# Filter taps folded about the middle of n1, with the filter's first transform stage in four 64x64 tiles

## The chip, the cores and the metric

The kernel runs on one core of one Trainium2 chip. The metric is the device time of one execution in microseconds. Before the change it is 1558.56 us, the median of three runs (1558.08 to 1559.79).

## The reference

Three layers follow one another. The first is a long convolution with a filter that a small network makes; two feed-forward layers work on its result. Only the first one is touched here.

```python
h_mlp = np.maximum(pos_emb @ w1, 0.0) @ w2          # 12480 x 128
h_filt = h_mlp * np.exp(-0.01 * np.arange(S))[:, None]
u = x * v
L = 2 * S
y = np.fft.irfft(np.fft.rfft(u, n=L, axis=1) * np.fft.rfft(h_filt, n=L, axis=0)[None], n=L, axis=1)[:, :S]
x = x * y                                            # then two layers of 128 -> 2048 -> 128
```

## The kernel before, in words

A sequence position is n1 * 128 + n2. The filter has weight only at its first 82 values of n1 (NH = 82), the data at 98. The transform over n1 is a matrix multiply with cosines and sines at 90 frequencies (K1 = 90). The channels are worked on in two groups g of 64. The program up to the feed-forward layers is written out in a fixed order, which every engine's queue keeps:

1. **Filter layers** (`layer1` L450, `layer2` L464, the loop at L477). `layer1` takes six values j of n2 (a *chunk*; 11 chunks, the last of four): two TensorE calls of 492 columns, one for each half q of n2 on 64 rows of the array each (L455), then two VectorE operations with relu and window for the two halves (L458) and a GpSimd add that makes their sum (L462) into `rh`. `layer2` takes four j: eight calls, 64 rows deep, 82 values of n1 wide, 128 columns (L469), then two ScalarE copies out of PSUM (L471), to `hf` for group 0 and to `ht` for group 1. One or two `layer2` follow each `layer1`. `make_u` (L400, L403) is work on the data: one VectorE product and two sums for each of 16 blocks; two of the blocks are done between layers.
2. **first(0, 1, i)**, 16 turns (L560): the filter's first stage of group 0. A turn has eight calls of 64 weight columns and 180 moving columns (L568), in two column tiles q (64 columns of the array each), and one ScalarE copy of 720 values (L574) into `A`. Its moving operand `f1t` is the table `f1` with the window over n1, made by ScalarE at L486 after the last `layer2`. `ht` is stored to DRAM (`hsc`) behind the first turn, and the next seven `make_u` are issued between turns.
3. **first(0, 0, i)**, 16 turns, the same for the data; then the second stage of group 0 (L596 to L635: `xp`, product, `gp`), 23 blocks.
4. **first(1, 0, i)**, 16 turns; `hf` is loaded back from `hsc` behind turns 4, 7, 10, 13 (L711). **first(1, 1, i)**, 16 turns on it. Then the second stage of group 1, 23 blocks, and the feed-forward layers, which take the rest of the time.

`feed(n)` runs n steps of the conversion of the four weight matrices (L516 to L539: VectorE and ScalarE work; loads `wk<-ws`): one step in a block of the second stage, two in a turn of first(1, .).

An fp32 call of TensorE is two passes: it leaves two LDWEIGHTS and two MATMUL rows in the trace, which stand next to each other in the program, on the same part of the array. A pass of two calls that sit on different halves of the array is called a *round* below. PSUM holds three buffers of two banks in turn (`bank_b`), so TensorE is at most three tiles ahead of ScalarE or VectorE.

## Time and profile before

| | |
|---|---|
| median of 3 runs | 1558.56 us |
| profiled execution, its own time | 1559.5 us |
| its span in the trace | 1557.7 us |
| busy: PE, VectorE, ScalarE, GpSimd | 98%, 91%, 84%, 86% of the span |
| mean granted TensorE clock | 0.992 |
| instructions | 22611 |

The shares of busy time are averages over stages with different limits: the feed-forward layers fill the last four fifths of the span and hold most of each sum. What the change is worth has to be read in the stretches that it touches, which all lie in the first 266 us.

### The profile page before, as it was taken

To read this page: it belongs to the slowest core of one execution; us is meant where nothing else is said; L and a number is where in the kernel's file an instruction comes from. 1 tells how busy PE (TensorE), PEld (TensorE's weight loads), DVE (VectorE), ACT (ScalarE), POOL (GpSimd) and SP (SyncE) were. 2 spreads that over 40 slices of the span, in tenths; PEclk is the share of its full clock that TensorE was granted. 3 is DMA by queue.
4 is the path that set the end of the run, shared out by engine and by line. 5 is a ranking of instruction groups with operands and counts; after the bars stand their busy time and mean duration, and the time that the engine had idled before them with its cause. 6 is when DMAs were issued, how large, how long until landed. Compare 5 with 4: busy or idle time off the path is not lost.

```text
span 1557.7 us, 22611 instructions
## 1 busy us (share of the span) xinstructions
PE 1519.0 (98%) x7248; PEld 1047.7 (67%) x7248; DVE 1418.9 (91%) x2387; ACT 1314.1 (84%) x2532; POOL 1344.1 (86%) x1167
## 2 busy tenths in 40 slices
PE   7999998899999999999999999999999999999999
PEld 5887787776666666666666666666666666666665
DVE  6488786799999999999999999999999999999992
ACT  4633732689999999999999999999999999999995
POOL 5087075799999999999999999999999999999993
PEclk9999999899999999999999999999999999999999
DMA  8784854871110111001110100000000000000000
GB/s 238 202 254 157 218 173 159 195 150 32 29 34 7 35 35 28 24 18 35 34 28 15 27 14 13 1 14 13 14 11 9 7 7 7 7 7 0 7 7 13
DMA packets 79709, 88.74 MB, mean 57 GB/s; under 512 B 51728, under 2 KB 59506, under 8 KB 78934
## 3 DMA queue, kind: packets, MB, share of 16 engines
q1 hardware_dynamic: 79590, 87.29, 20.5%
q8 instruction: 57, 0.93, 0.3%
q14 instruction: 62, 0.51, 0.1%
HBM read 66.39 MB, written 20.88 MB: 56 GB/s over the span
## 4 chain that ended last, share of the span: by engine, by line
PE 59%; POOL 19%; DVE 13%; issue 4%; ACT 3%; DMA 2%; SPq 1%; DVEq 0%; POOLq 0%; ACTq 0%
PE o1p L876 12%; PE o2p L876 9%; POOL wk L912 9%; PE h L434 7%; PE h L435 7%; PE h L436 7%; PE xp L600 4%; PE ap L568 4%; POOL wk L903 4%; POOL wk L905 3%; PE gp L624 3%; DVE v L914 3%; PE yP L828 3%; DVE g L927 2%; DVE wk L909 2%
## 5 line engine op out<-in xcount | busy, mean ns | idle before, releaser
L912 POOL TENSOR_TENSOR wk<-wk 128x972 f32<-128x972 f32 (+2 forms) x208 | 470.6, 2262 | 36.2 <-DVE wk L909 35.1
L876 PE MATMUL o1p<-g,u 128*128 128x486 f32 (+2 forms) x832 | 384.6, 569 | 1.4 <-DVE g L927 1.1
L903 POOL TENSOR_SCALAR wk<-wk,pars 128x486 f32<-128x486 f32 (+2 forms) x416 | 315.8, 760 | 19.7 <-ACT wk L895 19.1
L914 DVE SCALAR_TENSOR_TENSOR v<-wk,absb,v 128x486 f32<-128x486 f32 (+2 forms) x416 | 296.9, 714 | 4.7 <-ACT v L897 4.3
L876 PE MATMUL o2p<-wk,u 128*128 128x486 f32 (+2 forms) x624 | 296.7, 565 | 0.0
L921 DVE SCALAR_TENSOR_TENSOR v<-v,u 128x486 f32<-128x486 f32 (+2 forms) x416 | 273.4, 657 | 13.4 <-ACT u L919 13.0
L897 ACT ACTIVATE v<-h,absb 128x486 f32<-128x486 f32 (+2 forms) x416 | 262.5, 645 | 17.3 <-DVE g L927 15.5
L909 DVE TENSOR_TENSOR wk<-h,wk 128x486 f32<-128x486 f32 (+2 forms) x416 | 270.5, 650 | 1.1
L924 DVE SCALAR_TENSOR_TENSOR v<-v,u 128x486 f32<-128x486 f32 (+2 forms) x416 | 262.9, 658 | 3.3
L919 ACT ACTIVATE u<-u 128x486 f32<-128x486 f32 (+2 forms) x416 | 253.6, 610 | 6.8
L927 DVE TENSOR_TENSOR g<-wk,v 128x486 f32<-128x486 f32 (+2 forms) x416 | 256.2, 648 | 2.5 <-POOL wk L912 1.1
L934 ACT ACTIVATE wk<-h 128x486 f32<-128x486 f32 (+2 forms) x416 | 239.6, 577 | 20.2 <-PE o2p L876 9.5
L895 ACT ACTIVATE wk<-h 128x486 f32<-128x486 f32 (+2 forms) x416 | 239.0, 575 | 19.2 <-PE h L436 15.5
L917 ACT ACTIVATE u<-v 128x486 f32<-128x486 f32 (+2 forms) x416 | 239.5, 576 | 10.5 <-DVE v L914 2.7
L434 PE MATMUL h<-zh,wh 128*128 128x486 f32 (+2 forms) x416 | 237.3, 571 | 5.5 <-ACT rh L936 2.9
L905 POOL TENSOR_SCALAR wk<-wk,pars 128x972 f32<-128x972 f32 (+2 forms) x208 | 240.1, 1154 | 0.0
L434 PE MATMUL h<-uh,wh 128*128 128x486 f32 (+2 forms) x416 | 230.2, 553 | 1.5 <-DVE wk L909 0.9
L876 PEld LDWEIGHTS o1p<-g,u 128*128 128x128 f32 x832 | 152.7, 189 | 88.4 <-DVE g L927 34.7
L435 PE MATMUL h<-zl,wh 128*128 128x486 f32 (+2 forms) x416 | 159.4, 383 | 0.0
L436 PE MATMUL h<-zh,wl 128*128 128x486 f32 (+2 forms) x416 | 159.0, 382 | 0.0
L436 PE MATMUL h<-uh,wl 128*128 128x486 f32 (+2 forms) x416 | 158.0, 380 | 0.0
L435 PE MATMUL h<-ul,wh 128*128 128x486 f32 (+2 forms) x416 | 158.0, 380 | 0.0
(86 smaller groups left out, 2176.8 us busy)
## 6 DMA issues: line engine op xcount, KB each, us to landing
bd<-wk SPq DMA_DIRECT2D x44, 256.0 KB
bt<-bd SPq DMA_DIRECT2D x100, 112.5 KB
wk<-c_m SPq DMA_DIRECT2D x43, 256.0 KB
dt<-c_d SPq DMA_DIRECT2D x25, 344.5 KB
wk<-ws SPq DMA_DIRECT2D x16, 512.0 KB
u<-xu SPq DMA_DIRECT2D x16, 384.0 KB
wk<-vu SPq DMA_DIRECT2D x12, 384.0 KB
xt<-xm SPq DMA_DIRECT2D x13, 243.0 KB
```

Source lines behind the costliest of these rows:

```text
L434: pe.matmul(dst, w_h, z_h, start=start, stop=False)
L435: pe.matmul(dst, w_h, z_l, start=False, stop=False)
L436: pe.matmul(dst, w_l, z_h, start=False, stop=stop)
L876: pe.matmul(o, wo[l][:, f], T.pop((src, n))[:, :w], start=(f == 0), stop=(f == NF - 1))
L903: pool.tensor_scalar(out=q, in0=sq, scalar1=a3, scalar2=a1, op0=ALU.mult, op1=ALU.add)
L905: pool.tensor_scalar(out=new("p", n, 2)[:, : 2 * w], in0=T["s", n][:, : 2 * w], scalar1=a2, scalar2=a0, op0=ALU.mult, op1=ALU.add)
L909: dve.tensor_tensor(out=half("nn"), in0=one("h1"), in1=two("q"), op=ALU.mult)
L912: pool.tensor_tensor(out=nn, in0=nn, in1=T["p", n][:, : 2 * w], op=ALU.add)
L914: dve.scalar_tensor_tensor(out=one("v"), in0=two("s"), scalar=bb, in1=one("v"), op0=ALU.mult, op1=ALU.add)
L921: dve.scalar_tensor_tensor(out=one("v"), in0=one("v"), scalar=C1, in1=one("r0"), op0=ALU.add, op1=ALU.mult)
L924: dve.scalar_tensor_tensor(out=one("v"), in0=one("v"), scalar=-2.0, in1=one("r0"), op0=ALU.add, op1=ALU.mult)
L927: dve.tensor_tensor(out=mk("g"), in0=two("nn"), in1=one("v"), op=ALU.mult)
```

## The change

In the filter layers the 82 taps in n1 are folded about their middle: `z` holds taps n1 = 0..40 and, in reversed order, 81..41; `rh` gets for each j 41 sums (cosine part) and 41 differences (sine part), and 23 zero columns behind them. For that the half q = 1 is windowed first, the half q = 0 is added in the second VectorE operation; GpSimd scales the reversed half in place and adds (two operations of 246 values where one had 492); VectorE subtracts, one chunk later (`fold`). `layer2` becomes 32 calls of 64 columns, for sums and differences s, halves q, and channel halves a, each on one 64x64 quarter of the array (rows by q, columns by a). `first(., 1, i)` becomes 16 calls of 90 columns on 41 rows, in the four quarters (rows by a, columns by q). The window over n2 is taken out of the layers and given to the copy out of PSUM as a scale for each partition (`wr`). `f1t` is loaded as a table; the memsets of `f1t` and of the lower rows of `hf` go, one of the 23 zero columns comes. `hsc` is stored and loaded by 48 rows for each half of the partitions: 96 x 32 KB instead of 82 x 32 KB. The feed runs 1 or 2 steps (24 instead of 32 in all) in first(1, 1), and seven blocks of the second stage of group 1 have a second one.

```diff
-        w2n, w1n = (win[:, : N2 // 2], win[:, N2 // 2 : N2]), win[:, N2:]
+        r1 = [cut(Aw, o + 1792 + 512 * i, [6, NH]) for i in range(2)]
+        wj, wn, wr = win[:, :64], win[:, 64 : 64 + HH], win[:, 64 + HH :]
...
+        sp.dma_start(f1t, I["c_ft"])
         sp.dma_start(f1, I["c_f1"])
...
-        dve.memset(f1t, 0.0)
-        for c in range(0, DG, 16):
-            pool.memset(hf[64:, c : c + 16], 0.0)
+        pool.memset(rh[:, :, NH:], 0.0)
...
-            tmp, dst = r0[c // PB % 3][:, :n], rh[:, c : c + n]
-            for q, t in ((0, tmp), (1, dst)):
+            z, y, dst = r0[c // PB % 3][:, :n], r1[c // PB % 2][:, :n], rh[:, c : c + n]
+            for q, t, b, alu in (
+                (1, y, wj[:, c : c + n].unsqueeze(2).to_broadcast([128, n, NH]), ALU.mult), (0, z, y, ALU.add),
+            ):
                 dve.scalar_tensor_tensor(
-                    out=t, in0=qt[:, q, : n * NH].rearrange("p (j n) -> p j n", j=n), scalar=0.0,
-                    in1=w2n[q][:, c : c + n].unsqueeze(2).to_broadcast([128, n, NH]), op0=ALU.max, op1=ALU.mult,
+                    out=t, in0=qt[:, q, : n * NH].rearrange("p (j n) -> p j n", j=n), scalar=0.0, in1=b,
+                    op0=ALU.max, op1=alu,
                 )
-            pool.tensor_tensor(out=dst, in0=dst, in1=tmp, op=ALU.add)
+            za, zb = z[:, :, :HH], z[:, :, HH:]
+            pool.tensor_tensor(out=zb, in0=zb, in1=wn.unsqueeze(1).to_broadcast([128, n, HH]), op=ALU.mult)
+            pool.tensor_tensor(out=dst[:, :, :HH], in0=za, in1=zb, op=ALU.add)
+            fold()
+            odd.append((dst[:, :, HH:NH], za, zb))
+
+        def fold():
+            while odd:
+                dst, za, zb = odd.pop()
+                dve.tensor_tensor(out=dst, in0=za, in1=zb, op=ALU.subtract)

         def layer2(c):
-            hps = bank_b([2, 4, D], f"hps{c}")
+            hps = bank_b([2, 2, 4, DG], f"hps{c}")
             for i in range(4):
-                for q in (0, 1):
-                    h = slice(64 * q, 64 * q + 64)
-                    pe.matmul(hps[:NH, q, i], rh[h, c + i], w2b[h], start=True, stop=True)
+                for s in (0, 1):
+                    for q in (0, 1):
+                        for a in (0, 64):
+                            h = slice(64 * q, 64 * q + 64)
+                            pe.matmul(
+                                hps[a : a + 64, q, s, i], rh[h, c + i, s * HH : s * HH + 64], w2b[h, a : a + 64],
+                                start=True, stop=True,
+                            )
...
-        act.activation(f1t[:NH], f1[:NH], AF.Copy, scale=w1n[:NH])
...
         def first(g, s, i):
+            for e in (0, 1) if s else ():
+                for r, cols in ((0, (0, 2)), (1, (1, 0))):
+                    for q in (0, 1):
+                        k = slice(cols[q] * K1, cols[q] * K1 + K1)
+                        for a in (0, 1):
+                            p = slice(64 * a, 64 * a + HH)
+                            pe.matmul(
+                                ap_[64 * q : 64 * q + 64, 2 * a + e, r * K1 : r * K1 + K1],
+                                hf[p, 2 * q + (q ^ r), 2 * i + e], f1t[p, k], start=True, stop=True,
+                            )
...
-            act.copy(dst, a)
+            if s:
+                act.activation(dst, a, AF.Copy, scale=wr)
+            else:
+                act.copy(dst, a)
...
-                for c in range(0, DG, 16):
-                    spread(sp, hsc[:, c : c + 16], ht[:NH, c : c + 16])
+                for c in range(4):
+                    for a in (0, 64):
+                        sp.dma_start(hsc[a : a + HP, c], ht[a : a + HP, c])
...
-            feed(2)
+            feed(1 + i % 2)
...
-            feed(1)
+            feed(1 + (b % 4 == 1))
```

In the lists below the change's own lines are numbered as in its file: L464 is the old L455, L493 the old L469, L597 and L605 the old L568, L410 and L413 the old L400 and L403.

On TensorE at the end of the layers and the start of first(0, 1, .) (`qt` is the tile of a `layer1`, `hps` of a `layer2`, `ap` of a `first`; the columns are output partitions x columns and the number of calls), before:

```order
L455 MATMUL qt_323<-A 128x328 x2
L469 MATMUL hps_329<-A 82x128 x8
L469 MATMUL hps_340<-A 82x128 x8
L469 MATMUL hps_357<-A 82x128 x8
L469 MATMUL hps_368<-A 82x128 x8
L568 MATMUL ap_1_0_383<-f1t,wk 64x180 x8
```

and with the change:

```order
L464 MATMUL qt_627<-A 128x328 x2
L493 MATMUL hps_635<-A 64x64 x32
L493 MATMUL hps_671<-A 64x64 x32
L493 MATMUL hps_712<-A 64x64 x32
L493 MATMUL hps_747<-A 64x64 x32
L597 MATMUL ap_1_0_785<-f1t,wk 64x90 x16
```

The tiles keep their places; a `layer2` has four times as many calls of half the columns, a turn of the filter's first twice as many of half the columns.

On VectorE at the same place (the last two chunks and the first blocks of `make_u`), before:

```order
L458 SCALAR_TENSOR_TENSOR A<-qt_289,win 128x492 x2
L400 TENSOR_TENSOR wk<-wk,u_83 98x1024
L403 TENSOR_TENSOR u_83<-wk 98x8x64 x2
L458 SCALAR_TENSOR_TENSOR A<-qt_323,win 128x328 x2
L400 TENSOR_TENSOR wk<-wk,u_83 98x1024
L403 TENSOR_TENSOR u_83<-wk 98x8x64 x2
```

and with the change:

```order
L469 SCALAR_TENSOR_TENSOR A<-qt_543,win 128x492
L469 SCALAR_TENSOR_TENSOR A<-qt_543,A 128x492
L484 TENSOR_TENSOR A<-A 128x6x41
L410 TENSOR_TENSOR wk<-wk,u_83 98x1024
L413 TENSOR_TENSOR u_83<-wk 98x8x64 x2
L469 SCALAR_TENSOR_TENSOR A<-qt_627,win 128x328
L469 SCALAR_TENSOR_TENSOR A<-qt_627,A 128x328
L484 TENSOR_TENSOR A<-A 128x6x41
L484 TENSOR_TENSOR A<-A 128x4x41
L410 TENSOR_TENSOR wk<-wk,u_83 98x1024
```

A subtraction (L484) stands behind the two window operations of the next chunk; that of the second last chunk now stands behind the first `make_u` and the last chunk's two operations, and both last ones ahead of the second `make_u`.

On the DMA queue of SP where `hf` is loaded back, before (bd is the store of the second stage):

```order
L641 DMA bd<-wk 128x256
L311 DMA wk<-hsc 80x2048
L313 DMA wk<-hsc 2x2048
L504 DMA wk<-ws 128x1024
L311 DMA wk<-hsc 80x2048
```

and with the change:

```order
L681 DMA bd<-wk 128x256
L753 DMA wk<-hsc 48x4x512 x2
L532 DMA wk<-ws 128x1024
L753 DMA wk<-hsc 48x4x512 x2
L532 DMA wk<-ws 128x1024
```

The four loads keep their places among the loads of the weights; each has 96 rows in pieces of 512 values instead of 82 rows of 2048.

## Rows read from the trace of the kernel before

**Rows 1.** Busy time by stage, layers to second stage of group 1; columns named in the second line.

```profile
core 0: us, PE busy (x) PEld busy (x) DVE busy (x) ACT busy (x) POOL busy (x), PEclk, DMA share, GB/s
4.05:35.34 31.29, 26.85 (x301) 18.89 (x301) 22.06 (x32) 17.11 (x33) 18.83 (x14) 0.94 0.92 250
35.34:56.40 21.06, 21.06 (x258) 19.10 (x260) 11.84 (x15) 11.39 (x15) 0.00 (x0) 0.93 0.97 269
56.40:76.98 20.58, 19.67 (x258) 17.98 (x254) 10.45 (x13) 12.91 (x17) 0.00 (x0) 1.00 0.66 153
...
172.01:197.04 25.03, 21.72 (x257) 18.83 (x257) 19.63 (x38) 17.27 (x27) 0.00 (x0) 0.93 0.69 194
197.04:266.45 69.41, 67.08 (x306) 57.72 (x306) 51.50 (x84) 22.63 (x47) 50.99 (x66) 1.00 0.51 169
```

**Rows 2.** Timeline of TensorE in the layers: start, length, engine, line, shape, count.

```profile
15.51 1.96 PE L469 MATMUL hps<-A 64*82 64x128 f32 x32
...
18.09 1.07 PE L469 MATMUL hps<-A 64*82 64x128 f32 x16
...
19.79 1.97 PE L469 MATMUL hps<-A 64*82 64x128 f32 x32
```

**Rows 3.** Timeline, only 35.33 to 35.36 us: what first(0, 1, 0) starts at once.

```profile
35.34 0.57 PE L568 MATMUL ap<-f1t,wk 128*64 128x180 f32 x2 [1.58 <-ACT f1t L486]
35.34 0.19 PEld L568 LDWEIGHTS ap<-f1t,wk 128*64 128x64 f32 x2 [1.95 <-ACT f1t L486]
```

**Rows 4.** Groups by line and shape, 0 to 77 us: count, busy us, mean ns, idle before.

```profile
L574 ACT COPY A<-ap 128x720 f32<-128x720 f32 x32 | 24.3, 759 | 17.3 <-PE ap L568 13.7 <-issue 2.8 <-DMA u<-xu 0.8
...
L403 DVE TENSOR_TENSOR u<-wk 98x512 f32<-98x512 f32 x24 | 17.0, 748 | 0.4
...
L462 POOL TENSOR_TENSOR A<-A 128x492 f32<-128x492 f32 x10 | 13.2, 1319 | 6.8 <-DVE A L458 6.7
L458 DVE SCALAR_TENSOR_TENSOR A<-qt,win 128x492 f32<-128x492 f32 x20 | 12.5, 665 | 12.0 <-DMA u<-xu 5.0 <-POOL A L462 4.0 <-PE qt L455 3.0
...
L486 ACT ACTIVATE f1t<-f,win 82x270 f32<-82x270 f32 x1 | 0.5, 526 | 0.0
```

**Rows 5.** The same view, 0 to 420 us and 262 to 270 us: shorter operations.

```profile
L630 ACT COPY wk<-gp 128x256 f32<-128x256 f32 x44 | 16.4, 372 | 32.5 <-PE gp L624 32.5
...
L614 POOL TENSOR_TENSOR wk<-wk 128x256 f32<-128x256 f32 x44 | 32.5, 738 | 3.4
...
L613 DVE TENSOR_TENSOR wk<-wk 128x128 f32<-128x128 f32 x1 | 0.3, 279 | 0.0
```

**Rows 6.** Timeline, the end of the layers: TensorE, GpSimd and ScalarE.

```profile
29.91 1.79 POOL L462 TENSOR_TENSOR A<-A 128x328 f32<-128x328 f32 x1 [2.04 <-DVE A L458]
...
31.75 2.00 PE L469 MATMUL hps<-A 64*82 64x128 f32 x16 [0.67 <-POOL A L462]
...
33.80 0.58 ACT L471 COPY wk<-hps 82x512 f32<-82x512 f32 x1 [1.61 <-PE hps L469]
...
34.76 0.53 ACT L486 ACTIVATE f1t<-f,win 82x270 f32<-82x270 f32 x1
```

**Rows 7.** Timeline of VectorE, the last blocks of make_u and the second stage's first product.

```profile
61.67 1.22 DVE L400 TENSOR_TENSOR wk<-wk,u 98x1024 f32<-98x1024 f32 x1 [0.88 <-DMA wk<-vu]
...
68.70 1.29 DVE L403 TENSOR_TENSOR u<-wk 98x512 f32<-98x512 f32 x2
79.63 1.29 DVE L607 TENSOR_TENSOR wk<-xp,wk 128x512 f32<-128x512 f32 x2 [9.64 <-ACT wk L602]
```

**Rows 8.** Timeline of VectorE and TensorE at the start of first(1, 1, .).

```profile
176.77 0.43 DVE L516 TENSOR_SCALAR wk<-wk 128x512 int32<-128x512 int32 x1 [3.26 <-DMA wk<-ws]
...
178.56 17.61 PE L568 MATMUL ap<-f1t,wk 128*64 128x180 f32 x208 [2.24 <-ACT A L574]
```

**Rows 9.** DMA issues by tensor, whole span: count, KB each.

```profile
hsc<-A SPq DMA_DIRECT2D x4, 640.0 KB
```

**Rows 10.** Timeline of TensorE in the feed-forward layers: the densest run of passes.

```profile
295.57 1.91 PE L828 MATMUL yP<-dt,bt 90*64 90x98 f32 x40
```

## The prediction

> **What bounds the kernel now.** I read the busy time by stage first, then the timelines where a stage hands over to the next, then the groups of equal operations for prices. All that the change touches lies before 266 us [rows 1]; the feed-forward layers behind it keep their order and should only start earlier or later.

> In the layers TensorE sets the pace: two chunks (two `layer1`, three `layer2`) take 19.79 - 15.51 = 4.28 us [rows 2], and VectorE needs only 2 x 2 x 0.665 = 2.66 us of that, GpSimd 2 x 1.32 [rows 4]. At the end TensorE waits: for GpSimd's add of the last chunk, 1.79 us beside `make_u`'s products [rows 6], then 1.58 us for ScalarE's `f1t` [rows 3]. In first(0, 1) and first(0, 0) TensorE is busy throughout (21.06 of 21.06 us, 19.67 of 20.58) while ScalarE works 11.39 and 12.91 [rows 1]. But in the same stretch the DMA engines are at 0.97 [rows 1] and `make_u` waits for its loads, still at 61.67; its last block ends at 68.70 + 1.29 = 70.0 us, and VectorE's first product of the second stage starts at 79.63 [rows 7]. So TensorE bounds here with 9.6 us of room before `make_u` does. First(1, 1) is different: VectorE waits 3.26 us for a weight load, ScalarE's conversion stands behind it in its queue, the copies behind that, and TensorE's fourth turn starts only at 178.56 [rows 8]; its remaining 13 turns take 17.61 us.

> **What a round costs.** Sixteen rows of a `layer2` more take 1.96 - 1.07 = 0.89 us [rows 2]: 8 rounds of 128 columns, 0.111 each. First(0, 0) has 128 rounds of 180 columns in 19.67 us [rows 1], 0.154 each. A line through both gives 0.059 us for 64 columns and 0.080 for 90 (estimates from these rows).

> Whether four quarters share a round no row shows; two halves do. At 35.34 two matmuls and two weight loads start in the same 0.03 us [rows 3]. A call's two passes stand next to each other in the program and need the same half, so the second start is the next call's, ahead of the first call's second pass: a pass that waits for its part of the array does not hold up the calls behind it. I take it that this holds for quarters. [...]

> **The change part by part**

> *Layers.* A `layer2` has 64 rows, 16 rounds of four: 16 x 0.059 = 0.94 us against 0.89, +0.05 x 16 = +0.8. VectorE's subtraction of 246 values lies between 0.279 (128 values) and 0.748 (512) [rows 4, 5], nearer the first, 0.4; GpSimd's two of 246 are near the 0.738 of 256 values [rows 5], 1.45 in place of 1.32. Both stay under a chunk's 2.14 us: nothing, beside TensorE; 0.5 once, since the first `layer2` needs a subtraction that is issued behind the second chunk's operations. At the end the second last chunk's subtraction stands behind `make_u` and the last chunk (VectorE's order above), about 1 us later than its `layer2` runs now; the last add is 164 values instead of 328. I set these equal, within -0.5 and +2. `f1t` goes: the first turn can start when `hf` is copied, 33.80 + 0.58 = 34.38, where it now starts at 35.34 [rows 3, 6]: -0.9. Together +0.4: first(0, 1) starts about where it does.

> *First(0, 1).* A turn on TensorE: 32 rows, 8 rounds of four, 0.64 us instead of 1.23. Then ScalarE's copy bounds. It is 0.759 us now [rows 4]; with a scale for each partition it may cost more: `f1t`'s activation with one took 0.526 us for 270 values [rows 4], a plain copy of 256 takes 0.372 [rows 5]. So between 0.76 and 0.91; I take 0.84, the middle. 16 x 0.84 = 13.4 us instead of 21.06: -7.7.

> *What is late next.* First(0, 0) keeps its 1.23 us a turn and ends 7.3 us earlier (-7.7 + 0.4), so the product at 79.63 would start at 72.3. `make_u` must be done by then. The store of `hsc` is 96 rows of 32 KB in place of 82 (80 of them are in [rows 9]), +0.45 MB, and `f1t` comes as 0.14 MB: 0.59 MB at 269 GB/s [rows 1] are 2.2 us for a queue that is full: 70.0 + 2.2 = 72.2. The two meet, so the 7.3 just holds; if the loads slip further, it shrinks us for us.

> *First(1, 1).* TensorE falls to 0.64 a turn, but ScalarE has 16 x 0.84 = 13.4 us of copies, and of the conversions' share (17.27 busy [rows 1] less 17 copies of 0.759, 4.4 us) 24/32, 3.3. The stall ahead of it is a DMA matter: `hf` comes back with 0.45 MB more through a queue at 194 GB/s [rows 1], of which three quarters, 1.7 us, stand ahead of the load that VectorE waits for at 176.77 [rows 8]; and the first of its loads now touches all of `hf`'s place and waits for the last store of the second stage. 176.77 + 1.7 + 0.43 (VectorE's step) + 13.4 + 3.3 = 195.6, against 197.04; I leave 0.4 for small waits: -1.0, between -3 (copy at 0.76, no later load) and +2.

> *Second stage of group 1.* Eight feed steps move there, one more in each of seven blocks, in 69.41 us on 23 blocks, TensorE 67.08 busy and VectorE 51.50 [rows 1]. 8 steps of at most 0.75 us (512 values [rows 4]) fit into 18 us idle; at the start, where blocks follow without `gp`, one delays a product: +0.5, at most 2.

> **The sum** for the profiled execution: +0.4 - 7.7 - 1.0 + 0.5 = -7.8: 1559.5 - 7.8 = 1551.7. The median of the runs is 0.94 below that execution: **1550.8 us**. A change of 0.2%, 3.1 us, is about what a measurement of this kernel can tell from none.

> **The rivals**

> 1. *Two at a time (slower).* The quarters don't share a round: rows and columns don't combine, or passes go in order. A `layer2` is then 32 rounds of 0.059 = 1.89 us, +1.0 x 16 = +16; a turn of the first 16 x 0.080 = 1.28, no gain; with `f1t` gone +15 in all: 1574. From a `layer2` of 1.4 us on (+0.5 x 16 = 8) the change loses. For it: no row shows four. Against it: rows 3. Chance 0.10.

> 2. *Supply of passes (slower).* The change has 16 x (64 - 16) + 32 x 16 = 1280 more rows each of loads and matmuls. The densest run here is 40 in 1.91 us, 0.048 each [rows 10]; it was not bound by supply (98 columns a pass), so this is a bound from above. At that price a `layer2` is 3.1 us, +2.2 x 16 = +35, a turn 1.53, +0.3 x 32 = +10: 1603. If weight loads of two column quarters took turns, as much as one round of that run (0.095), `layer2` would be 1.5 us and the sum +2. Chance 0.06 for slower.

> 3. *Gain absorbed.* The loads for `make_u` land 5 us later instead of 2 (each waits for the block four before it, and `make_u`'s second block starts later), the stall in first(1, 1) grows by 3 us, so that 0 to 3 us are left: 1555.6 to 1558.6. For it: DMA at 0.97 and waits on it in rows 7 and 8. Against it: DMA falls to 0.66 behind 56 us [rows 1]. The change's TensorE time would then be as forecast, the second stage's first product at 75 or later. Chance 0.15.

> **How the numbers follow.** The forecast keeps 0.69: gains of 3.1 to 12. Its ends: the copy at 0.76 (-1.3 twice), first(1, 1) at -3, layers at -0.5 make -12, 1546.6; layers +2, `make_u` +2, first(1, 1) +2, the blocks +2 leave about 1555. The range reaches over rival 3 and a little beyond: 1546.5 to 1561, which leaves out rivals 1 and 2 and some 0.03 below: 0.81. Faster 0.69, same 0.13 (most of rival 3), slower 0.18 (rivals 1 and 2, 0.02 of rival 3).

> **What would show each step.** `layer2` of 64 rows in about 0.95 us and two chunks still in 4.3 to 4.5; first(0, 1) turns at the pace of ScalarE's copy, 0.76 to 0.91, with TensorE idle between them and its clock still granted at 1.00 once it is up (at the lower of its two levels a turn would be 1.3 us and this gain gone); the last `make_u` ends near 72 and the first product starts right behind it; first(1, 1) still opens with a wait for `wk<-ws`. A turn of 1.28 us with two starts at a time says rival 1; TensorE idle with "issue" between passes, rival 2; VectorE waiting for `wk<-vu` behind 70 us, rival 3.

## The result, and the profile after

The change makes the kernel 1.4% slower: 1581.3 us (median of four runs, 1579.25 to 1583.8) against 1559.17 in the same comparison, a ratio of 1.0137 (95% interval 1.0111 to 1.0162). The forecast was 1550.8, the range ended at 1561. The profiled execution has a span of 1579.6 us, 21.9 more than before.

Busy time by stage of the changed kernel, the stretches cut where TensorE's first call of each stage starts (layers, first(0, 1), first(0, 0), first(1, 0), first(1, 1), second stage of group 1; columns as in [rows 1]):

```profile
4.15:49.92 45.77, 36.00 (x1068) 23.35 (x1069) 23.83 (x40) 16.40 (x32) 15.86 (x22) 0.89 0.63 167
49.92:71.15 21.23, 17.45 (x513) 16.67 (x513) 12.18 (x15) 13.03 (x16) 0.00 (x0) 0.68 0.87 263
71.15:93.50 22.35, 21.44 (x259) 18.95 (x256) 12.50 (x15) 13.01 (x17) 0.00 (x0) 0.92 0.79 184
161.70:191.69 29.99, 26.16 (x274) 21.66 (x274) 16.97 (x32) 16.02 (x27) 2.04 (x4) 0.94 0.75 173
191.69:217.23 25.54, 19.45 (x512) 18.18 (x512) 16.40 (x31) 18.00 (x25) 0.00 (x0) 0.55 0.74 193
217.23:290.12 72.89, 71.23 (x318) 61.00 (x318) 57.60 (x91) 23.60 (x49) 53.24 (x66) 0.97 0.53 176
```

Against [rows 1]; its first(1, 0) and, cut at the same place, its second stage of group 1 were:

```profile
145.10:172.01 26.91, 24.52 (x274) 20.72 (x274) 16.99 (x32) 16.02 (x27) 2.05 (x4) 1.00 0.75 196
...
197.04:268.61 71.57, 69.20 (x318) 59.61 (x318) 52.13 (x85) 23.00 (x48) 50.99 (x66) 1.00 0.52 171
```

Two thirds of the loss are in the layers: 45.77 - 31.29 = +14.5. First(0, 1) takes 21.23 instead of 21.06, though its matmuls have half the columns: granted clock 0.68. First(0, 0), which was not touched, +1.8; first(1, 0) +3.1; first(1, 1) +0.5 at a clock of 0.55; the second stage of group 1 +1.3. The second stage of group 0 (68.2 against 68.1) and all behind 290 us (+0.3) are as before. Together 14.5 + 0.2 + 1.8 + 0.1 + 3.1 + 0.5 + 1.3 + 0.3 = 21.8; TensorE's first call is 0.1 later.

TensorE's timeline in the layers and in first(0, 1), with the idle time before each piece and its releaser:

```profile
4.15 5.81 PE L464 MATMUL qt<-A 64*128 64x492 f32 x12 [4.15 <-DMA A<-posT]
10.08 1.16 PE L493 MATMUL hps<-A 64*64 64x64 f32 x64
11.17 1.09 PE L464 MATMUL qt<-A 64*128 64x492 f32 x4
12.20 2.10 PE L493 MATMUL hps<-A 64*64 64x64 f32 x128
14.22 1.10 PE L464 MATMUL qt<-A 64*128 64x492 f32 x4
15.25 0.34 PE L493 MATMUL hps<-A 64*64 64x64 f32 x7
18.94 1.08 PE L493 MATMUL hps<-A 64*64 64x64 f32 x57 [3.36 <-issue]
19.95 1.98 PE L464 MATMUL qt<-A 64*128 64x492 f32 x4
21.86 1.90 PE L493 MATMUL hps<-A 64*64 64x64 f32 x65
25.10 1.16 PE L493 MATMUL hps<-A 64*64 64x64 f32 x63 [1.33 <-issue]
26.19 1.10 PE L464 MATMUL qt<-A 64*128 64x492 f32 x4
27.21 1.14 PE L493 MATMUL hps<-A 64*64 64x64 f32 x59
30.84 0.48 PE L493 MATMUL hps<-A 64*64 64x64 f32 x5 [2.48 <-issue]
31.25 2.01 PE L464 MATMUL qt<-A 64*128 64x492 f32 x4
33.19 3.69 PE L493 MATMUL hps<-A 64*64 64x64 f32 x128
...
51.70 2.86 PE L597 MATMUL ap<-f1t,wk 41*64 41x90 f32 x127 [0.79 <-issue]
57.44 13.78 PE L597 MATMUL ap<-f1t,wk 41*64 41x90 f32 x351 [2.88 <-issue]
```

TensorE stops in the middle of a `layer2`, waiting for nothing that the profile shows ("issue"). Count the matmuls between the stops: from 18.94 to the next one 57 + 4 + 65 = 126, then 63 + 4 + 59 = 126, and from 51.70 to 57.44 127. Each matmul has a weight load beside it, so that is 252 to 254 instructions; with the semaphore instructions that the kept trace has on TensorE between the same stops (4, 3 and 1), it is 256 each time. The page lists DMA traffic that is no data (queue, kind: packets, MB, share), after:

```profile
q8 instruction: 67, 1.10, 0.3%
```

Before, it had 57 packets and 0.93 MB: some 16.4 KB a packet in both. After, 8528 matmuls and 8528 loads are 254.6 for each packet; before, 2 x 7248 / 57 = 254.3. The profile doesn't say whose program a packet holds, but the count fits TensorE's in both kernels (a second queue of this kind, q14, has 62 packets and 0.51 MB in both). So does the time. Asked for 15.5 to 19 us alone, the DMA traffic has one such packet:

```profile
q8 instruction: 1, 0.02, 2.7%
```

Its rivals: "long chain" (the window, two GpSimd operations and the subtraction set the pace, and the label misleads) and "small quarters" (the calls of 64 and 90 columns cost more by themselves and keep the clock down).

### The profile page after: what moved, and what is told of

Same layout as the page of the kernel before. It is cut to its first block, busy times and chain, and to the rows that moved or that the text cites. A ratio compares the mean times of both kernels' runs of the same rounds, so it can differ in the third digit from the quotient of the medians.

```text
span 1579.6 us, 25188 instructions
## 1 busy us (share of the span) xinstructions
PE 1528.4 (97%) x8528; PEld 1053.7 (67%) x8528; DVE 1425.3 (90%) x2397; ACT 1316.1 (83%) x2531; POOL 1342.1 (85%) x1175
## 4 chain that ended last, share of the span: by engine, by line
PE 61%; POOL 18%; DVE 11%; issue 4%; ACT 4%; DMA 2%; SPq 0%; POOLq 0%; DVEq 0%; ACTq 0%
PE o1p L917 12%; PE o2p L917 9%; POOL wk L953 9%; PE h L443 7%; PE h L444 7%; PE h L445 7%; PE xp L640 5%; PE gp L664 3%; POOL wk L944 3%; POOL wk L946 3%; PE yP L869 3%; DVE v L955 3%; DVE g L968 2%; DVE wk L950 2%; DVE v L962 2%
```

## The experiments

**late_loads**: the loads of x and v, and the `make_u` in the layers, behind the layers.

```diff
-        for c in range(VB + 2):
-            load_x(c)
-            if c < VB:
-                load_v(c)
...
+        for c in range(4):
+            for a in (0, 64):
+                sp.dma_start(hsc[a : a + HP, c], ht[a : a + HP, c])
+        for c in range(VB + 2):
+            load_x(c)
+            if c < VB:
+                load_v(c)
```

> The changed kernel with the loads of x and v (and their two make_u) put behind the filter layers; the same TensorE instructions in the same order. Theory 'pages': TensorE's instructions arrive in pieces of 256 (126 or 127 matmuls lie between two stops with 'issue'), the next piece is asked for while the last one runs, and behind the loads it queues for up to 6 us. Then, with nothing else on the DMA engines, the three stops before 31 us (3.36, 1.33 and 2.48 us) shrink to under 1.2 us each, and first(0, 1, 0) starts between 37 and 43 us instead of 49.92, though every layer2 has its 32 calls. Theory 'long chain' (window, two GpSimd operations, subtraction set the pace and the label 'issue' misleads): the stops stay where they are and first(0, 1, 0) starts at 46 to 50. Theory 'small quarters' (the calls of 64 columns themselves cost more, and keep the clock down): a layer2 still takes 1.05 us or twice that, the stops don't matter, start at 46 or later. The loads now come late, so the total is longer in any case, 1585 to 1610, and decides nothing.

First(0, 1, 0) starts at 41.45 us. TensorE's timeline:

```profile
27.25 0.45 PE L484 MATMUL hps<-A 64*64 64x64 f32 x11 [0.66 <-issue]
27.63 1.10 PE L455 MATMUL qt<-A 64*128 64x492 f32 x4
28.66 1.16 PE L484 MATMUL hps<-A 64*64 64x64 f32 x64
29.75 1.09 PE L455 MATMUL qt<-A 64*128 64x492 f32 x4
30.77 2.09 PE L484 MATMUL hps<-A 64*64 64x64 f32 x128
32.80 0.82 PE L455 MATMUL qt<-A 64*128 64x328 f32 x4
...
35.11 2.09 PE L484 MATMUL hps<-A 64*64 64x64 f32 x127 [0.76 <-issue]
39.10 1.62 PE L484 MATMUL hps<-A 64*64 64x64 f32 x93 [1.91 <-issue]
```

The stops of 3.36, 1.33 and 2.48 us are gone from their places; what is left are 0.66, 0.76 and 1.91, at later ones. The same instructions are through 8.5 us earlier (49.92 - 41.45), of which 1.26 are the last subtraction's wait behind `make_u`, because of transfers that TensorE doesn't wait for: the chain isn't the bound, and the supply depends on what else the DMA engines carry (a share of 0.63 over the layers in the change, 1.02 from 10 to 29 us; 0.22 over the layers here). Undisturbed, two chunks take 32.80 - 27.63 = 5.17 us, 0.89 over the 4.28 of [rows 2]: a `layer1` 1.02 from start to start (before 0.83), a single `layer2` 1.09 (before 0.88), two 2.03 (1.76). The total, 1592.45 in one run, holds the late loads.

**quarters_of_128**: `layer2` in 16 calls of 128 columns, rows by q and columns by sum or difference, crossed; first(., 1) as dense as in the change.

```diff
-                        for a in (0, 64):
-                            h = slice(64 * q, 64 * q + 64)
-                            pe.matmul(
-                                hps[a : a + 64, q, s, i], rh[h, c + i, s * HH : s * HH + 64], w2b[h, a : a + 64],
+                        h = slice(64 * q, 64 * q + 64)
+                        pe.matmul(
+                            hps[64 * (s ^ q) : 64 * (s ^ q) + 64, q, i], rh[h, c + i, s * HH : s * HH + 64], w2b[h],
```

> The changed kernel with the quarters of layer2 chosen by q (rows) and by sum or difference (columns), crossed for q = 1, and not by halves of the channels: 16 calls of 128 columns instead of 32 of 64, so 64 instructions in place of 128; first(., 1) keeps its 16 calls of 90 columns in four quarters, with the row half as real or imaginary part. The arithmetic is that of the change. Theory 'pages': the layers need 4.3 pieces of 256 instructions instead of 8.5, each lasting over 5 us; a layer2 is four rounds of 128 columns, 0.45 to 0.5 us; two chunks take 3.5 us (VectorE: four window operations and two subtractions); first(0, 1, 0) starts at 31 to 36 us; first(0, 1, .) is as dense as in the change and still runs short, 15 to 21 us for 16 turns; first(1, 1, .) likewise. Total 1550 to 1562, the changed kernel's 22 us gone. Theory 'long chain': the chain is the same, first(0, 1, 0) starts at 44 to 50, total 1575 or more. Theory 'small quarters': rounds as slow as in the change or the clock down for most of the layers, start at 38 to 44, total 1568 to 1576.

1568.28 us, ratio 1.0048 (1.003 to 1.0067): two thirds of the loss gone, not all. First(0, 1, 0) starts at 38.54, with one stop left in the layers (2.15 us at 33.35). Start and total lie in the ranges of "small quarters", not of "pages". My price for its `layer2` was wrong by two: 16 calls are 32 passes (x32, 1.03 us from start to start), so 8 rounds and not 4, 1.0 us and not 0.45, which is 9 us over 16 of them. So this run doesn't decide between the two. First(0, 1) takes 19.1 us: 3.67 for the first five turns (0.73 each), a stop of 2.03, then 13.47 for eleven (1.22 each) at a lower clock, which lasts into first(0, 0), 24.0 (granted clock 0.60 in 40 to 60 us, 0.89 in 60 to 80). And first(1, 0) is back at 26.93; it loads the same bytes of `hf` as the change, in pieces of 8 KB instead of 2 KB.

**old_first**: the change's layers, with first(., 1) in 8 calls of 180 columns (the two halves of the channels are no longer kept apart, so only its times count).

```diff
+            for i_ in range(4) if s else ():
+                for q in (0, 1):
+                    pe.matmul(
+                        ap_[64 * q : 64 * q + 64, i_, : 2 * K1], hf[:, 2 * q + i_ % 2, 2 * i + i_ // 2],
+                        f1t[:, q * K1 : (q + 2) * K1], start=True, stop=True,
+                    )
```

> The changed kernel's layers as they are, with first(., 1, .) made of 8 calls of 180 columns on 128 rows as before (half the calls of the change; the two halves of the channels are summed wrongly, so the filter's spectrum isn't the reference's). Theory 'pages': the layers are those of the change (first(0, 1, 0) at 48 to 51 us), first(0, 1, .) takes 21 to 22 us without a stop marked 'issue' and with the clock at 1.00 once it is up; total 1578 to 1584, no more than 3 us from the change, since the quarters of the first stage gave nothing there. If the quarters of first(., 1) themselves cost time (theory 'small quarters'), the total falls by 5 us or more. Theory 'long chain': as 'pages'; this run doesn't tell those two apart.

1575.26 us in one run, 6.0 under the change: more than "pages" allowed, and what "small quarters" forecast. But 2.4 of it lie in the layers, which have the same instructions and took 43.38 us here instead of 45.77, with shorter stops: they differ that much from run to run. First(0, 1) starts at 47.46 and takes 19.57 us with TensorE busy throughout and a clock of 1.00, where the change takes 21.23 at 0.68. So the quarters of the first stage lose time here too, 1.7 us, and as much by what they leave behind in first(0, 0) (22.35 against 20.61); whether by themselves or by the supply, this run doesn't say.

**before_32col**: the kernel before, each `layer2` call cut into four of 32 columns.

```diff
-                    pe.matmul(hps[:NH, q, i], rh[h, c + i], w2b[h], start=True, stop=True)
+                        pe.matmul(
+                            hps[:NH, q, i, e : e + 32], rh[h, c + i], w2b[h, e : e + 32], start=True, stop=True
+                        )
```

> The kernel before with each call of layer2 cut into four calls of 32 columns: as many instructions as the changed layer2 (128), no folding, no quarters, the same chain of VectorE and GpSimd as before, the same result. Theory 'pages': stops marked 'issue' appear in the layers, 126 or 127 matmuls (or a multiple) apart, of 1 to 3.5 us while the loads run; the layers end 6 to 16 us later than before (first(0, 1, 0) at 41 to 51 instead of 35.34), and the total grows by 5 to 15 us. Theory 'long chain' and theory 'small quarters': no such stops, layers longer only by what 32 columns cost more than a quarter of 128 (a layer2 of 1.0 to 1.5 us instead of 0.89 to 1.07), first(0, 1, 0) at 35 to 40.

1615.07 us in one run, far beyond all three. TensorE's timeline:

```profile
4.17 3.71 PE L455 MATMUL qt<-A 64*128 64x492 f32 x8 [4.17 <-DMA A<-posT]
8.47 1.10 PE L455 MATMUL qt<-A 64*128 64x492 f32 x4 [0.59 <-DMA A<-posT]
9.40 2.47 PE L470 MATMUL hps<-A 64*82 64x32 f32 x64
11.70 1.07 PE L455 MATMUL qt<-A 64*128 64x492 f32 x4
12.61 4.82 PE L470 MATMUL hps<-A 64*82 64x32 f32 x128
17.26 1.07 PE L455 MATMUL qt<-A 64*128 64x492 f32 x4
18.17 0.42 PE L470 MATMUL hps<-A 64*82 64x32 f32 x8
20.11 3.21 PE L470 MATMUL hps<-A 64*82 64x32 f32 x56 [1.52 <-issue]
...
24.90 9.09 PE L470 MATMUL hps<-A 64*82 64x32 f32 x128
```

The first stop comes after 8 + 4 + 64 + 4 + 128 + 4 + 8 = 220 matmuls; in the changed kernel, with other operands, other tiles and another chain, after 12 + 64 + 4 + 128 + 4 + 7 = 219. That is a place in the program, not in the work. Of the several stops that "pages" forecast, this is the only one. The rest I had not foreseen: behind this one stop the granted clock falls to 0.50 and stays there, 0.53 in 20 to 40 us and 0.50 up to 88, while TensorE is busy (20.00 of the 20 us from 40 to 60). The calls of 32 columns then take twice as long (128 in 9.09 us, ahead of the stop in 4.82), and no second stop follows: a piece lasts 9 us.

**layer2_8calls**: as quarters_of_128, with sums and differences in one call of 105 weight columns: as many calls as before the change.

```diff
-            rows(np.exp(rate * N2 * (NH - 1 - 2 * h1))), np.tile(np.exp(rate * (63 - j)), 2)[:, None],
+            np.outer(np.repeat([1.0, -1.0], FO), np.exp(rate * N2 * (NH - 1 - 2 * h1))), np.tile(np.exp(rate * (63 - j)), 2)[:, None],
...
+                    pe.matmul(hps[:NR, q, i], rh[h, c + i], w2b[h], start=True, stop=True)
```

> As quarters_of_128, with layer2 in as many instructions as before the change (8 calls, 128 columns, 105 weight columns: sums in output rows 0 to 40 and differences in 64 to 104, for q = 1 the other way round, by a sign in the window table), and the waiting subtraction issued ahead of make_u. First(., 1, .) keeps its 16 calls in quarters. Theory 'pages': the layers need no more pieces of 256 instructions than before, so no stop marked 'issue' over 0.5 us in the layers up to the last three layer2; a layer1 behind a layer2 costs 0.83 us again from start to start instead of 1.02 (no change between halves and quarters of the array), two chunks 4.2 to 4.5 us instead of 5.0 to 5.2; first(0, 1, 0) starts at 34 to 37 us. First(0, 1, .) is as dense as in the change and still runs short: one or two stops, 16 to 21 us. Total 1555 to 1563. Theory 'long chain' (two window operations, two of GpSimd, a subtraction): the same chain, first(0, 1, 0) at 42 or later. Theory 'small quarters' (the calls of 64 columns themselves): layers as under 'pages', so this run doesn't tell those two apart in the layers; in first(0, 1, .) the clock is low even without a stop ahead of it.

1569.05 us, ratio 1.0041 (1.0021 to 1.006). First(0, 1, 0) starts at 36.20, with the change's whole chain (the last subtraction moved ahead of `make_u`) and no "issue" in the layers: "long chain" falls, and most of the layers' 14.5 us is gone. A `layer1` is 0.83 to 0.88 us from start to start again, two chunks 4.38: the 0.2 us each time go with the quarters beside it. The total is above the 1555 to 1563 forecast. First(0, 1) takes 19.5 us, with a stop of 2.43 and 13.48 us at the lower clock behind it (0.57 in 40 to 60 us):

```profile
36.20 3.67 PE L591 MATMUL ap<-f1t,wk 41*64 41x90 f32 x161 [0.68 <-ACT wk L492]
42.31 13.48 PE L591 MATMUL ap<-f1t,wk 41*64 41x90 f32 x351 [2.43 <-issue]
```

First(1, 0) takes 32.3 us here; its loads have rows in 32 + 9.

**turns_alternate** and **turns_in_pairs**: as layer2_8calls, turns of first(0, 1) and first(0, 0) mixed, one by one or two by two.

```diff
-        for i in range(16):
-            first(0, 0, i)
...
+            if i > 1:
+                first(0, 0, i - 2)
```

> As layer2_8calls, with the turns of first(0, 1, .) and first(0, 0, .) issued alternately (the second two turns behind) instead of one group of 16 after the other; the ten make_u between them. Theory 'pages': a pair of turns has 96 instructions in about 2.1 us, so 256 of them last 5.5 us, and next to no stop is left; the clock comes up within the first turns and stays; both stages together take 33 to 38 us instead of 41.6 before; the second stage's first call starts at 69 to 74 us instead of 76.98. Total 1550 to 1557. Theory 'small quarters': the quarters' calls keep the clock down whatever stands between them: both stages 42 us or more, total 1562 or more. If each change between quarters and whole columns of the array costs 0.2 us (as layer1 behind layer2 suggests), 32 of them take 6 us back: both stages 39 to 42, total 1556 to 1560.

> As turns_alternate, with two turns of first(0, 1, .) and two of first(0, 0, .) in turn, so that half as many changes of shape are left: 16 instead of 32. Theory 'pages': within 1.5 us of turns_alternate, either way. If a change of shape costs 0.2 us: 2 to 4 us faster than turns_alternate. If the supply is still short inside two dense turns (128 instructions in 1.5 us), stops marked 'issue' come back and it is slower by 2 us or more.

1601.25 and 1581.02 us: both far slower than forecast, for a reason I had overlooked. TensorE stands still for 17.35 and 16.02 us after the first turns, behind the copies of first(0, 0). By the code, these write the half of `A` that holds `ht`, which has to be stored first; that was not tried by itself. In pairs, TensorE's timeline behind the stop:

```profile
62.93 1.47 PE L591 MATMUL ap<-f1t,wk 41*64 41x90 f32 x64
...
66.92 1.47 PE L591 MATMUL ap<-f1t,wk 41*64 41x90 f32 x64
```

Four turns take 66.92 - 62.93 = 4.0 us (before 4.9; granted clock 0.94 in 60 to 80 us, 1.00 in 80 to 100), with stops of 1.20 and 0.66 behind them; one by one, the turns behind the stop run at 0.50 from 60 to 100 us, a pair of them in 4.0 us instead of 2.15 ahead of it. So mixing thins the instructions as meant, but with `ht` in this place (if the code is read rightly) it doesn't pay.

**first_unloaded**: as layer2_8calls, every load of x and v and the store of `ht` behind the last turn of first(0, 1).

```diff
+        sp.dma_start(hf[:, 63, 120:128], I["c_e"][:, 0, :8])
+        for c in range(0, DG, 16):
+            for a in (0, NR - 48):
+                sp.dma_start(hsc[a : a + 48, c : c + 16], ht[a : a + 48, c : c + 16])
```

> As layer2_8calls, with every load of x and v and the store of the filter's second half put behind the last turn of first(0, 1, .) (a small load into the filter's place waits for it), so that the DMA engines are idle in the layers and in all of first(0, 1, .); TensorE's instructions and their order stay. A piece of 256 instructions holds four turns. Theory 'pages': with the queue empty a piece comes every 3.5 to 4.0 us (the distance of the stops in late_loads at 35.11 and 39.10 us was 3.99), so first(0, 1, .) takes 14 to 16.5 us instead of 19.5, in stops of under 1 us each or none, and the clock stays up or falls only in part. Theory 'small quarters' (the calls keep the clock down by themselves, stops or not): 16 turns at 1.2 us, 18 to 20 us, with the granted clock near 0.5 in most of it. The loads come some 17 us late, so the total is 1585 to 1610 and decides nothing.

First(0, 1) takes 13.16 us, less than the 14 to 16.5 forecast. The layers and first(0, 1) by stage, then TensorE's timeline in first(0, 1), then the DMA traffic of the same stretch (the digits are 40 equal slices of 0.33 us):

```profile
4.07:32.61 28.54, 26.28 (x301) 18.46 (x301) 17.86 (x33) 16.13 (x32) 14.97 (x22) 1.00 0.30 101
32.61:45.77 13.16, 11.62 (x512) 10.82 (x512) 0.00 (x0) 11.60 (x16) 0.00 (x0) 1.00 0.02 5
```

```profile
32.61 6.67 PE L578 MATMUL ap<-f1t,wk 41*64 41x90 f32 x289 [0.88 <-ACT wk L483]
39.95 2.86 PE L578 MATMUL ap<-f1t,wk 41*64 41x90 f32 x128 [0.67 <-issue]
43.68 2.09 PE L578 MATMUL ap<-f1t,wk 41*64 41x90 f32 x95 [0.87 <-issue]
```

```profile
DMA  0002000000000020000000000200000000001000
...
q8 instruction: 4, 0.07, 2.2%
```

This settles it. Nothing but instructions moves; the four packets lie 11 slices apart, 3.6 us, and the stops lie 128 matmuls, 3.73 us, apart. The second and the third packet start at 37.2 to 37.6 and 40.9 to 41.2 us by the slices and take 1.2 us in the mean (2.2% of 16 engines over 13.2 us, four packets), so they end ahead of the stops, which begin at 39.28 and 42.81, and the stops end some 1.2 to 1.7 us behind them. Four turns at a clock of 1.00 are 2.86 us (0.715 each), so even with no other transfers the supply sets the pace; but the stops are short, and the clock stays at 1.00. "Small quarters" falls as the reason why the clock goes down: the same calls keep it up here. (What quarters cost by themselves in the layers, some 4 us, stands in the next section; that they didn't bring the clock back once it was down, in the last.) The 1591.99 us of its one run hold the loads that came late.

**rows_48**: as layer2_8calls, 48 rows from 0 and 48 from 57 in the store and the loads of `hsc`.

```diff
-                    spread(sp, hf[a : a + HH, c : c + 16], hsc[a : a + HH, c : c + 16])
+                    sp.dma_start(hf[a : a + 48, c : c + 16], hsc[a : a + 48, c : c + 16])
```

> As layer2_8calls, with the filter's second half stored and loaded as 48 rows from row 0 and 48 rows from row 57 (in place of 32 and 9 rows from 0 and from 64), in pieces of 8 KB. If the 5.4 us that first(1, 0, .) takes longer in layer2_8calls than before (32.3 against 26.9) are the DMAs of 9 rows, they go (quarters_of_128, with 48 rows in pieces of 8 KB, has 26.9, the changed kernel with 48 rows in pieces of 2 KB 30.0): first(1, 0, .) in 26.5 to 27.5 and a total 4 to 6 us under layer2_8calls, within 0.3% of before. If it is the later start of the stage or the conversion's own chain, it stays at 30 or more. Theory 'pages' for the rest: first(0, 1, .) still 19 to 20 us, no gain over before of more than 2 us in the total, since a piece of 256 instructions (four turns) comes no faster than the four turns of before's pace.

1563.3 us (twelve runs, 1556.81 to 1570.82), ratio 1.0023 (1.0006 to 1.0041); first(1, 0) takes 27.4 us, as forecast. By the ratios the total is 0.18%, 2.8 us, under layer2_8calls, not the 4 to 6 forecast; first(0, 1) takes 21.48, not 19 to 20. TensorE's timeline in first(0, 1), DMA share 0.92:

```profile
37.99 3.67 PE L591 MATMUL ap<-f1t,wk 41*64 41x90 f32 x161 [0.68 <-ACT wk L492]
44.09 5.07 PE L591 MATMUL ap<-f1t,wk 41*64 41x90 f32 x128 [2.44 <-issue]
50.29 5.08 PE L591 MATMUL ap<-f1t,wk 41*64 41x90 f32 x128 [1.12 <-issue]
55.66 3.88 PE L591 MATMUL ap<-f1t,wk 41*64 41x90 f32 x95 [0.30 <-issue]
```

Under load the stops lie 6.20 and 5.37 us apart, in place of 3.73. Four turns before the change took 4.9 us: with these loads running, the pieces of 256 instructions, four turns each, came no faster than that, whatever the array did. No version of mine beats the kernel before.

## Why the prediction was wrong, by its own steps

**What held.** Quarters share rounds: a turn in 0.715 us (forecast 0.64; one that goes two at a time would be 1.28), a pair of `layer2` in 2.03 (1.88; 3.8). In the kept trace four matmuls start within 0.02 us (51.70 to 51.72), the next four 0.1 later. Of the last three ahead of the stop that ends at 30.84, two start at 28.08 and one at 28.14, which fits a call's second pass that waits for its quarter while the next call goes ahead. Rival 1 is out, and with it passes in order. ScalarE's scaled copy takes 0.862 us (0.84 taken, 0.76 to 0.91 allowed), the subtraction 0.404 (0.4), GpSimd's two 0.760 + 0.702 (1.45). First(0, 1), priced at 13.4 us, takes 13.16 where nothing disturbs the supply, but that it comes so close is luck: the copies overlap there (nine in 6.87 us, 0.76 each and not 0.84), and 0.67 + 0.87 us of it are stops, which the sum did not have. The forecast's upper end was added up wrongly: -7.7 with +2 four times is +0.3, some 1559 and not "about 1555"; the range to 1561 held that too.

**The step that failed first: "Layers", +0.4; measured +14.5.** It priced what the array does and took the passes as supplied. The runs showed that they are not: instructions come in pieces of 256, every 3.7 us where nothing else moves (first_unloaded), and two `layer2` are through one in 2.1. Stops marked "issue" are 3.36 + 1.33 + 2.48 + 0.48 = 7.65 us of it. The quarters' own cost is some 4: eight `layer1` at +0.19, five single `layer2` at +0.21 and five and a half pairs at +0.27 by the differences under late_loads (the forecast had 0.05 a `layer2` and nothing for `layer1`; a second `layer2` in a row, 2.03 - 1.09 = 0.94, is as forecast, so the rest goes with the alternation of `layer1` and `layer2`). The lower clock behind the stops is about 4.4: from start to start 1.94 instead of 1.02 at 31.25 and 3.62 instead of 2.03 at 33.19 (granted clock 0.50), 1.91 instead of 1.02 at 19.95 (0.52) and some 0.9 in the pair at 21.86 (0.58). The first three `layer1` take 0.45 longer. The waits at the end are shorter, 1.26 + 0.73 against 1.39 + 0.67 + 1.58 before: -1.7. These estimates make 14.9, 0.4 more than was measured.

**"First(0, 1)", -7.7; measured +0.2.** The turn was sized right and could not be had: two stops, 0.79 and 2.88, then eleven turns in 13.78 us, 1.25 each, at the lower clock (0.50 from 57.57 to 74.64 us). The prediction had named that level and its price (1.3 us a turn, "this gain gone"), as a sign and not as a case with a chance. The low clock runs on into first(0, 0), +1.8, which the sum did not have.

**"First(1, 1)", -1.0; measured +0.5, and +3.1 ahead of it.** The clock is at 0.55 here, behind waits of 2.11, 1.35 and 2.12 us for ScalarE's copies and one stop of 1.09, so that the last nine turns take 1.23 us each. Of the 3.1, 1.6 are a stretch at the lower clock ahead of any load of `hf` (0.62 from 163.07 to 167.56; the first load is issued at 173.6), which the sum did not have either. The delay of the loads (taken as 1.7 us, by bytes) falls in first(1, 0) behind it and goes with the size of the pieces: its last 13 turns take 172.28 to 191.69, 19.41 us, with 2 KB, 17.98 with 8 KB and the same bytes, 17.96 before. **"Second stage of group 1", +0.5; measured +1.3**, with the clock at 0.97 instead of 1.00.

**The rivals.** Rival 2 named the mechanism and the sign ("TensorE idle with 'issue' between passes"), with a chance of 0.06. Its price was of the wrong kind: 0.048 us a row from a run of 40 [rows 10], too short to reach the end of a piece. What counts is how long 256 instructions last. Before, it was 31.29 / 301 x 128 = 13 us in the layers and 10.5 in first(0, 1) [rows 1], against some 6 us of supply under load (6.20 and 5.37 in rows_48). By the forecast's own prices two `layer2`, 128 rows of each kind, were to last 2 x 0.94 = 1.9 us. Rival 3 is not what happened: there was no gain to absorb. The loads fill the DMA engines up to 29 us (share about 1.0 from 10 on) and are done behind 31 (0.03 up to 46), while the layers go on; what they do is to delay the instructions, by 8.5 us as late_loads shows.

## What to carry to other kernels

Before cutting calls smaller, divide: how long do 256 instructions of TensorE last after the change, and how often do instruction packets come when the DMA engines are as busy as there. Here it was 2.1 to 2.9 us against 3.7 alone and up to 6.2 under load, and the smaller calls bought stops. The long stop in first(0, 1) cost twice, 2.88 us and then eleven turns in 13.78 us, which at 0.715 each are 7.9, and another 1.8 in first(0, 0), so count the stage after it too. And look at what the label hides: "issue" says only that the profile shows no wait, and the count of matmuls from one stop to the next said more.

## What the runs showed that I had not expected

- A stop has a place in the program: after 219 and 220 matmuls in two different kernels, then every 126 to 128 (or a multiple: 377 from 30.84 to 44.13 us in the change).
- The clock, once down behind a stop, stayed down through long busy stretches of small calls: 13.78 us in first(0, 1) of the change (0.51), and from 20 to 88 us in before_32col (0.53 and 0.50). In first_unloaded, stops of 0.67 and 0.87 us did not bring it down (1.00). It did not rise again within a first(., 1) on quarters: in the change it is at 0.50 from 57.57 to 74.64 and from 194.11 to 221.41 us, past the end of both, in quarters_of_128 at 0.50 from 180 to 200, and the eleven turns behind the stop in first(0, 1) take 13.47 us there and 13.48 in layer2_8calls. With calls of 180 columns it did: first(1, 1) has waits of some 2 us near its start before, in old_first and in the change, and its clock is 0.93 [rows 1], 0.94 and 0.55. So "small quarters" is right in this half: the calls didn't bring the clock down here, but they didn't bring it back either. Why is not settled by these runs.
- A `layer1` takes 1.02 us from start to start between calls on quarters of the array, 0.83 to 0.88 between calls on halves. That it is the change from one to the other that costs these 0.2 us was not tried by itself, and it is not so everywhere: in turns_in_pairs four turns with two changes take 3.99 us, where two of 0.715 and two of 1.23 are 3.89.
- The form of a load: the 13 turns of first(1, 0) in which `hf` is loaded take 19.41 us with pieces of 2 KB and 17.98 with 8 KB, 21.71 with rows in 32 + 9 (the last three of them in 5.56, 1.85 each) and 18.42 with 48. The other 1.6 us by which the whole stage is longer in the first of each pair are a stretch at the lower clock (0.62), ahead of the loads; why it falls there is open.
